# Four small edits to the first head pair and to the minimum of the last queries

## The chip, the core and the metric

The kernel runs on one core of a Trainium2 chip. The metric is the device time of one execution in microseconds (us). The engines are TensorE (PE, with its weight loads as PEld), VectorE (DVE), ScalarE (ACT), GpSimd (POOL) and SyncE (SP, which issues the transfers).

## What is computed

The reference has three stages, in float32. Attention over 4 batches, 8 heads, 1152 positions and head size 64, in which the queries are averaged in pairs, so that 576 queries are left; then a layer of four causal attention experts with a gate that keeps two of four; then a gated convolution layer.

```python
q_pool = q.reshape(B, H, S // 2, 2, D).mean(axis=3)
scores = scale * np.matmul(q_pool, k.transpose(0, 1, 3, 2))
scores = scores - np.max(scores, axis=-1, keepdims=True)
attn = np.exp(scores)
attn = attn / (np.sum(attn, axis=-1, keepdims=True) + 1e-09)
x = np.matmul(attn, v)                      # then (B, 576, 512)
for e in range(4):                          # experts, Hd = 64
    a = softmax(causal(scale * (x @ wq[e]) @ (x @ wk[e]).T))
    out += gate[e] * (a @ (x @ wv[e]) @ wo[e])
gate2 = sigmoid(causal depthwise convolution of out, 5 taps)
return (gate2 * (out @ w_val)) @ w_out
```

## The kernel before

**Order.** Every engine runs its instructions in the order in which the code issues them; there is no scheduler. The first stage follows a string of letters (`ORDER`, line 425) once per pair of heads: S is one piece of scores, T the transposes of a third of a tile, R a row minimum, X an exponential, H the shares, A the product with V. Lists of closures (`late`, `preps`, `begin`) put other work between these.

**First stage.** Sixteen pairs of heads (4 batches x 4) are taken one after the other. A pair has nine tiles of 128 query rows: four for each head and one mixed tile that holds the last 64 queries of both heads. A tile's scores are 128 x 1152 in three groups of 384 keys (`GW`). Each operand is split into a high part, rounded to float32r, and a low part, the rest; `ka` and `kb` (`kst`) hold the keys of the pair's two heads with both parts. For a tile, `scores` (line 436) makes the matmuls (line 451), `rowmin` (line 453) the minimum of the negated scores on VectorE, `expo` (line 458) the exponential with its sum on ScalarE, `transp` (line 492) the transposes (line 500) and their copies (lines 508 and 510), and `av` (line 512) the product with V (line 530), followed by the multiplication with the shares. There are two score buffers, so a tile's scores wait for the exponential two tiles before.

**The first pair** has no pair before it and is prepared in `first()` (line 544) and in the plain loop of line 707. Its queries and keys come twice over, for each head on all partitions (`q0`, `k0`). `qload` and `kload` issue the transfers on SyncE, in this order: for head 0 the queries' first half, the first 384 keys, the other 768 keys; the same for head 1; then the queries' second halves. `kpart(h, g, eng)` makes the high part of a key group on ScalarE (line 584) and the low part on `eng` (line 585). Head 0's three groups are done with VectorE for the low parts; head 1's in `second()` with GpSimd, which is called after the first row minimum. `third()` goes on with the queries' second halves on GpSimd. Before all of this, ScalarE fills parts of two small tiles with zeros (line 347), from a tile that GpSimd sets, and TensorE runs spare matmuls (`spin`, line 617).

**The shares.** After the last exponential of a half of a pair's tiles, `shares` (line 465) adds a small number to the row sums (line 472), takes reciprocals (line 473) and leaves a closure `copies` at the head of `late`. It spreads the reciprocals over 64 or 128 columns of the tile `rm` (lines 478 and 480), which `spread_shares` transposes on TensorE (line 489) at the start of `av`. The copies are made by GpSimd, but for the first half of the first pair by VectorE.

**Second stage.** For each of 4 batches and 2 pairs of experts there are five tiles; `scores2` (line 814) makes the scores, masks them (line 834) and takes the minima (line 835). Tiles 0 to 3 hold 128 queries, and their two banks are the two experts, so two minima are wanted. Tile 4 holds the last 64 queries of both experts (128 rows); its two banks are the two halves of the keys, and a further instruction (line 837) takes the smaller of the two minima. `expo2` (line 839) reads column 0 of `nm` for tile 4. `norm2` (line 850) multiplies the exponentials with the shares on GpSimd (lines 861 and 866).

Of the kernel before, what the change touches and what calls it, by code (L numbers as in the profile page):

```python
# [12 lines left out]
AF = mybir.ActivationFunctionType  # L13
ALU = mybir.AluOpType
AX = mybir.AxisListType
# [5 lines left out]
def tile_kernel(ctx, tc, q, k, v, w_gate, wq, wk, wv, wo, w_val, conv_w, w_out, wo_t, q0, k0, out):  # L21
    nc = tc.nc
    B, H, S, D = v.shape
    P = 128
# [10 lines left out]
    pe, act, dve, pool = nc.tensor, nc.scalar, nc.vector, nc.gpsimd  # L35
# [28 lines left out]
    def f(ap):  # L64
        return ap.bitcast(F32)
# [256 lines left out]
    G = 3  # L322
    GW = 3 * P
# [4 lines left out]
    with ExitStack() as s1:  # L328
# [136 lines left out]
        def shares(m):  # L465

            n, u, i, _ = tiles[m]
            k = len(UNITS[u])
            if i == k - 1:
                rs = st_p.tile([P, 5], F32, name="rs")[:, 0:k]  # L470
                rm = rss[n, u] = rb_p.tile([P, 3, P], F32, name="rm")
                dve.tensor_scalar(rs, sums[(2 * n + u) % len(sums)][:, 0:k], 1e-9, None, op0=ALU.add)
                dve.reciprocal(rs, rs)  # L473
                both = rs[:, 0:4].rearrange("p (h t) -> p t h", h=2)[:, :, :, None].to_broadcast([P, 2, 2, D])

                def copies():
                    eng = pool if n or u else dve
                    eng.tensor_copy(rm[:, 0:2].rearrange("p t (h d) -> p t h d", d=D), both)  # L478
                    if u == 0:
                        eng.tensor_copy(rm[:, 2], rs[:, 4:5].to_broadcast([P, P]))  # L480

                late.insert(0, copies)

# [60 lines left out]
        def first():  # L544

            bufs = pt_p.tile([P, C, 2, 256], F32, name="pt1").rearrange("p c h q -> p (c h q)")
            bufs = [bufs[:, i * S:(i + 1) * S] for i in range(4)]
            kd, qd = bufs[0:2], [t.rearrange("p (c r q) -> p c r q", c=2, r=2) for t in bufs[2:4]]
            vn = v_p1.tile([P, 2, C, D], F32, name="vn")
            kst = [kst_p.tile([P, 2, C * P], F32R, name=n) for n in ("ka", "kb")]  # L550
            data[0] = [qst[0], kst, vn, None]
            def qload(h, c):
                nc.sync.dma_start(qd[h][:, c], q0[h, :, c])

            def kload(h, a, z):
                nc.sync.dma_start(kd[h][:, a:z], k0[h, :, a:z])

            for h in range(2):
                qload(h, 0)
                kload(h, 0, GW)  # L560
                kload(h, GW, S)
            for h in range(2):
                qload(h, 1)

            def qadd(h, c, eng):
                eng.tensor_tensor(out=qd[h][:, c, 0], in0=qd[h][:, c, 0], in1=qd[h][:, c, 1], op=ALU.add)

            def pieces(h, c):
                qp = qd[h][:, c, 0]
                if c == 0:  # L570
                    return [(qst[0][h][:, 0:HQ], qp)]
                return [(last0[h][:, 64 * h:64 * h + 64], qp[:, 4 * P - HQ:]), (qst[0][h][:, HQ:], qp[:, 0:4 * P - HQ])]

            def qhigh(h, c):
                for hi, qp in pieces(h, c):
                    act.activation(hi, qp, AF.Copy, scale=-scale / 2)

            def qlow(h, c, i=0):
                hi, qp = pieces(h, c)[i]
                dve.scalar_tensor_tensor(out=hi[64:P], in0=qp[64:P], scalar=-scale / 2, in1=f(hi[64:P]), op0=ALU.mult, op1=ALU.subtract)  # L580

            def kpart(h, g, eng):
                gs = slice(g * GW, (g + 1) * GW)
                act.activation(kst[h][:, 0, gs], kd[h][:, gs], AF.Copy)
                eng.tensor_tensor(out=kst[h][:, 1, gs], in0=kd[h][:, gs], in1=f(kst[h][:, 0, gs]), op=ALU.subtract)  # L585

            def second():
                kpart(1, 0, pool)
                qhigh(1, 0)
                for g in range(1, G):  # L590
                    kpart(1, g, pool)
                qlow(1, 0)

            def third():
                qadd(1, 1, dve)
                qadd(0, 1, pool)
                for i in range(2):
                    for h in range(2):
                        hi, qp = pieces(h, 1)[i]
                        pool.tensor_scalar(hi, qp, -scale / 2, None, op0=ALU.mult)  # L600

            qadd(0, 0, dve)
            qhigh(0, 0)
            qlow(0, 0)
            kpart(0, 0, dve)

            def rest():
                for g in range(1, G):
                    kpart(0, g, dve)
                qadd(1, 0, dve)  # L610

            return {-1: rest, 0: second, 1: third,
                    2: lambda: (qlow(0, 1), qlow(1, 1), qlow(0, 1, 1)), 3: lambda: qlow(1, 1, 1)}

# [114 lines left out]
        spread, bursts = iter(ends), iter(ends)  # L729
# [78 lines left out]
    with ExitStack() as s2l:  # L808
# [5 lines left out]
        def scores2(s):  # L814
            b, g, i = s
            d = live[s] = {}
            ps = d["ps"] = ps_s2.tile([P, 2, 512], F32, name="s")
            nm = d["nm"] = st_p2.tile([P, 2], F32, name="nm")
            sm = d["sm"] = st_p2.tile([P, 2], F32, name="sm")
            d["p"] = p_p2.tile([P, 2 * 4 * P], F32, name="p")  # L820
            if i < 4:
                w = (i + 1) * P
                for e in range(2):
                    for hl in range(2):
                        pe.matmul(ps[:, e, 0:w], lhsT=qs[g][e][:, i * P:(i + 1) * P], rhs=ks[g][e][:, hl, 0:w], start=hl == 0, stop=hl == 1)  # L825
                dg, mk = ps[:, :, i * P:w], cmask[:, None, :].to_broadcast([P, 2, P])
            else:
                w = HQ
                for c in range(2):
                    ops = [(e, hl) for e in range(2) for hl in range(2)]  # L830
                    for o, (e, hl) in enumerate(ops):
                        pe.matmul(ps[:, c, 0:w], lhsT=qs[g][e][:, 4 * P:], rhs=ks[g][e][:, hl, c * w:(c + 1) * w], start=o == 0, stop=o == 3)  # L832
                dg, mk = ps[:, 1, w - R64:w], cmask2
            dve.tensor_tensor(out=dg, in0=dg, in1=mk, op=ALU.max)
            dve.tensor_reduce(nm, ps[:, :, 0:w], axis=AX.X, op=ALU.min)  # L835
            if i == 4:
                dve.tensor_tensor(out=nm[:, 0:1], in0=nm[:, 0:1], in1=nm[:, 1:2], op=ALU.min)

        def expo2(s):
            b, g, i = s  # L840
# [171 lines left out]
        for n in range(len(steps) + LAG):  # L1012
            if n < len(steps):
                b, g, i = s = steps[n]
# [28 lines left out]
            t = 0.0  # L1043
# [28 lines left out]
            if n < len(steps):  # L1072
                scores2(s)
# [48 lines left out]
    with ExitStack() as s3:  # L1122
# [5 lines left out]
        both = gs_p.tile([P, KT, 2, 2 * SQ], F32R, name="gs")  # L1128
# [102 lines left out]
```

## Time and profile before

| what | value |
|---|---|
| median of 3 runs | 752.74 us (752.27 to 752.74) |
| the profiled execution, its time | 752.01 us |
| its span, first to last instruction | 750.2 us |
| PE busy | 742.2 us, 99% |
| DVE busy | 564.8 us, 75% |
| ACT busy | 447.7 us, 60% |
| POOL busy | 327.4 us, 44% |

Times inside the profile are counted from the span's start. Busy time is the union of an engine's instructions. The chain of work that ended last is followed backwards from the last instruction, at each step to what released it. A timeline row that says x2 joins two neighbouring instructions. The profile does not give each transfer's landing in the timeline; the view of a line gives the least, the median and the greatest time from issue to landing.

### The profile page before, as it was taken

To read this page: it belongs to the slowest core of one execution; us is meant where nothing else is said; L and a number is where in the kernel's file an instruction comes from. 1 tells how busy PE (TensorE), PEld (TensorE's weight loads), DVE (VectorE), ACT (ScalarE), POOL (GpSimd) and SP (SyncE) were. 2 spreads that over 40 slices of the span, in tenths; PEclk is the share of its full clock that TensorE was granted. 3 is DMA by queue.
4 is the path that set the end of the run, shared out by engine and by line. 5 is a ranking of instruction groups with operands and counts; after the bars stand their busy time and mean duration, and the time that the engine had idled before them with its cause. 6 is when DMAs were issued, how large, how long until landed. Compare 5 with 4: busy or idle time off the path is not lost.

```text
span 750.2 us, 14753 instructions
## 1 busy us (share of the span) xinstructions
PE 742.2 (99%) x5317; PEld 616.3 (82%) x5317; DVE 564.8 (75%) x1056; ACT 447.7 (60%) x985; POOL 327.4 (44%) x446
## 2 busy tenths in 40 slices
PE   8999999999999999999999999999999999999998
PEld 7787887787777877877877878889998879888887
DVE  6777898898988988866766667446788889868841
ACT  6666675665656656756657566424574554768442
POOL 6564675675667766743634611012322222336000
DMA  7976878778788597678458484359445553830212
GB/s 263 255 167 202 222 192 254 194 235 252 190 247 255 162 284 220 194 213 244 121 179 227 128 236 162 86 155 212 143 111 128 156 153 73 232 118 15 85 71 84
DMA packets 83784, 133.51 MB, mean 178 GB/s; under 512 B 19072, under 2 KB 55424, under 8 KB 83712
## 3 DMA queue, kind: packets, MB, share of 16 engines
q1 hardware_dynamic: 83712, 132.58, 62.2%
q8 instruction: 42, 0.69, 0.4%
q14 instruction: 30, 0.25, 0.1%
HBM read 53.37 MB, written 21.76 MB: 100 GB/s over the span
## 4 chain that ended last, share of the span: by engine, by line
PE 94%; DMA 2%; DVE 2%; ACT 1%; issue 0%; SPq 0%
PE s L451 21%; PE t L500 19%; PE t L530 19%; PE a L253 7%; PE o L1140 7%; PE a L286 4%; PE a L790 3%; PE a L925 3%; PE a L947 3%; PE s L825 3%; PE a L897 2%; DMA xh<-x_d 2%; PE t L489 1%; PE s L832 1%; PE a L781 1%; DVE nm L456 1%
## 5 line engine op out<-in xcount | busy, mean ns | idle before, releaser
L463 ACT ACTIVATE p<-s,nm 128x1152 f32<-128x1152 f32 x144 | 176.2, 1223 | 87.9 <-DVE nm L456 85.7
L456 DVE TENSOR_REDUCE nm<-s 128x1 f32<-128x1152 f32 x144 | 192.1, 1352 | 14.0 <-PE s L451 13.7
L500 PE MATMUL t<-ident,p 128*128 128x128 f32 x1296 | 199.0, 275 | 0.6 <-DVE xf L532 0.3
L500 PEld LDWEIGHTS t<-ident,p 128*128 128x128 f32 x1296 | 149.0, 141 | 26.5 <-ACT pt L508 7.1
L508 ACT ACTIVATE pt<-t 128x384 f32<-128x384 f32 x223 | 102.2, 490 | 79.8 <-PE t L500 74.9
L530 PE MATMUL t<-pt,vn 128*64 128x256 f32 (+1 forms) x1152 | 146.7, 408 | 0.1
L510 DVE COPY pt<-t 128x384 f32<-128x384 f32 x209 | 110.9, 554 | 44.6 <-PE t L500 40.7
L530 PEld LDWEIGHTS t<-pt,vn 128*64 128x64 f32 x1152 | 80.0, 137 | 56.0 <-issue 5.2
L451 PE MATMUL s<-ka,qst 128*128 128x384 f32 x384 | 114.7, 380 | 0.2 <-DVE ka L585 0.2
L451 PE MATMUL s<-kb,qst 128*128 128x384 f32 x384 | 99.1, 367 | 1.3 <-ACT p L463 1.3
L861 POOL TENSOR_TENSOR p<-p,sm 128x512 f32<-128x512 f32 (+3 forms) x32 | 40.1, 1254 | 101.4 <-DVE sm L859 63.3
L451 PEld LDWEIGHTS s<-kb,qst 128*128 128x128 f32 x384 | 60.9, 189 | 15.3 <-issue 13.1
L451 PEld LDWEIGHTS s<-ka,qst 128*128 128x128 f32 x384 | 62.9, 190 | 1.3 <-DVE ka L585 0.9
L478 POOL COPY rm<-rs 128x256 f32<-128x256 f32 x31 | 12.4, 399 | 79.0 <-DVE rs L473 77.8
L388 POOL TENSOR_TENSOR hlk<-kt,hlk 128x384 fp32r<-128x384 f32 x45 | 45.4, 1009 | 1.1
L532 DVE TENSOR_TENSOR xf<-t,rb 128x320 f32<-128x320 f32 (+1 forms) x32 | 14.6, 456 | 41.2 <-PE t L530 40.4
L539 POOL CAST xt<-xf 128x320 fp32r<-128x320 f32 (+1 forms) x32 | 13.6, 425 | 70.5 <-DVE xf L532 69.9
L253 PE MATMUL a<-xh,wqk 128*128 128x288 f32 x288 | 43.4, 299 | 0.7 <-DMA xh<-x_d 0.7
L846 ACT ACTIVATE p<-s,nm 128x256 f32<-128x256 f32 (+3 forms) x64 | 33.1, 526 | 16.2 <-DVE nm L835 16.2
L253 PEld LDWEIGHTS a<-xh,wqk 128*128 128x128 f32 x288 | 39.5, 188 | 2.0 <-DMA xh<-x_d 1.2
L226 DVE SCALAR_TENSOR_TENSOR gp<-x,cw,gp 128x572 f32<-128x572 f32 (+3 forms) x48 | 38.7, 810 | 2.7 <-ACT gp L950 2.1
L451 PE MATMUL s<-hlk,mixed 128*128 128x384 f32 x135 | 33.7, 357 | 0.0
(190 smaller groups left out, 1174.0 us busy)
## 6 DMA issues: line engine op xcount, KB each, us to landing
ka<-hlk SPq DMA_DIRECT2D x90, 192.0 KB, 3.2
kb<-hlk SPq DMA_DIRECT2D x90, 192.0 KB, 3.7
vn<-in_v_dram SPq DMA_DIRECT2D x16, 576.0 KB, 7.2
k<-hl SPq DMA_DIRECT2D x32, 288.0 KB, 4.9
kt<-in_k_dram SPq DMA_DIRECT2D x15, 576.0 KB, 6.1
qt<-in_q_dram SPq DMA_DIRECT2D x15, 576.0 KB, 5.3
qst<-hlq SPq DMA_DIRECT2D x60, 128.0 KB, 3.1
xh<-x_d SPq DMA_DIRECT2D x12, 576.0 KB, 6.6
```

The source lines that it names most:

```text
L226: dve.scalar_tensor_tensor(out=gp[:, n:], in0=x[:, 0:SQ - n], scalar=cw[:, m, c:c + 1], in1=gp[:, n:], op0=ALU.mult, op1=ALU.add)
L253: pe.matmul(ps[:, 0:HQ], lhsT=wqk[wi][:, t, cs], rhs=xh[t][xi][:, qsl], start=o == 0, stop=o == len(ops) - 1)
L388: late.append(lambda: pool.tensor_tensor(out=hlk[:, 1, gs], in0=kt[:, gs], in1=f(hlk[:, 0, gs]), op=ALU.subtract))
L451: pe.matmul(ps[:, 0:GW], lhsT=ops[c][0], rhs=ops[c][1], start=c == 0, stop=c == len(ops) - 1)
L456: dve.tensor_reduce(d["nm"], d["s"][:, :, 0:GW], axis=AX.XY, op=ALU.min)
L463: act.activation(d["p"], d["s"][:, :, 0:GW], AF.Exp, bias=d["nm"], scale=-1.0, accum_out=sums[(2 * n + u) % len(sums)][:, i:i + 1])
L500: pe.transpose(ps[:, j * P:(j + 1) * P], p[:, g, j * P:(j + 1) * P], ident)
L508: act.activation(dst, src, AF.Copy)
L510: dve.tensor_copy(dst, src)
L530: pe.matmul(ps[64 * h:64 * h + 64, 0:N], lhsT=vn[:, h, j, :], rhs=pt[:, j, h, :], start=j == 0, stop=j == C - 1)
L861: pool.tensor_tensor(out=pv, in0=pv, in1=sm[:, :, None].to_broadcast([P, 2, w]), op=ALU.mult)
L1140: pe.matmul(ps[:, 0:w], lhsT=hl[xi][:, kt, t * P - a:(t + 1) * P - a], rhs=end3["wo3"][:, kt, wi, c:c + w], start=o == 0, stop=o == len(op ...
```

## The change

Four edits. The first 384 keys of the first pair's head 0 are issued by ScalarE and not by SyncE, at the same place in the code. The high part of the last key group of head 1 is made by GpSimd and not by ScalarE: GpSimd now makes it after the low part of the group before the last two, and ScalarE makes two high parts there. The two copies of the shares in the first half of the first pair are made by ScalarE and not by VectorE. In the second stage the minimum of tile 4 is one reduction over both banks into column 0; the second instruction goes.

```diff
                 def copies():
-                    eng = pool if n or u else dve
-                    eng.tensor_copy(rm[:, 0:2].rearrange("p t (h d) -> p t h d", d=D), both)
+                    spread = [(rm[:, 0:2].rearrange("p t (h d) -> p t h d", d=D), both)]
                     if u == 0:
-                        eng.tensor_copy(rm[:, 2], rs[:, 4:5].to_broadcast([P, P]))
+                        spread.append((rm[:, 2], rs[:, 4:5].to_broadcast([P, P])))
+                    for dst, src in spread:
+                        if n or u:
+                            pool.tensor_copy(dst, src)
+                        else:
+                            act.activation(dst, src, AF.Copy)
...
             def kload(h, a, z):
-                nc.sync.dma_start(kd[h][:, a:z], k0[h, :, a:z])
+                queue = act if h == a == 0 else nc.sync
+                queue.dma_start(kd[h][:, a:z], k0[h, :, a:z])
...
             def second():
                 kpart(1, 0, pool)
                 qhigh(1, 0)
-                for g in range(1, G):
-                    kpart(1, g, pool)
+                pool.tensor_copy(kst[1][:, 0, 2 * GW:], kd[1][:, 2 * GW:])
+                kpart(1, 1, pool)
+                pool.tensor_tensor(out=kst[1][:, 1, 2 * GW:], in0=kd[1][:, 2 * GW:], in1=f(kst[1][:, 0, 2 * GW:]), op=ALU.subtract)
                 qlow(1, 0)
...
             dve.tensor_tensor(out=dg, in0=dg, in1=mk, op=ALU.max)
-            dve.tensor_reduce(nm, ps[:, :, 0:w], axis=AX.X, op=ALU.min)
-            if i == 4:
-                dve.tensor_tensor(out=nm[:, 0:1], in0=nm[:, 0:1], in1=nm[:, 1:2], op=ALU.min)
+            if i < 4:
+                dve.tensor_reduce(nm, ps[:, :, 0:w], axis=AX.X, op=ALU.min)
+            else:
+                dve.tensor_reduce(nm[:, 0:1], ps[:, :, 0:w], axis=AX.XY, op=ALU.min)
```

## Rows read from the trace of the kernel before

**Rows 1.** The page: span, busy time by engine, chain that ended last by engine.
```profile
span 750.2 us, 14753 instructions
...
PE 742.2 (99%) x5317; PEld 616.3 (82%) x5317; DVE 564.8 (75%) x1056; ACT 447.7 (60%) x985; POOL 327.4 (44%) x446
...
PE 94%; DMA 2%; DVE 2%; ACT 1%; issue 0%; SPq 0%
```

**Rows 2.** The chain that ended last, 0 to 60 us: start, length, what.
```profile
1.63 4.51 DMA pt<-in_k_dram
...
15.16 1.31 PE s L451 x6
```

**Rows 3.** Line 556, the four key transfers: issue durations (ns), starts; time to landing.
```profile
L556 SPq DMA_DIRECT2D pt<-in_k_dram x4: 416/428/432, 1.2 to 3.0; - x4
...
DMA to landing us min/median/max: 2.9/4.7/5.3
```

**Rows 4.** Timeline of ACT, 0 to 12 us: start, length, instruction, [idle before <- releaser].
```profile
2.87 0.40 ACT L347 ACTIVATE last<-zero 128x64 fp32r<-128x64 f32 x2 [0.88 <-POOL zero L62]
...
6.17 0.94 ACT L584 ACTIVATE ka<-pt 128x384 fp32r<-128x384 f32 x2 [1.23 <-DMA pt<-in_k_dram]
...
8.50 0.92 ACT L584 ACTIVATE kb<-pt 128x384 fp32r<-128x384 f32 x2
```

**Rows 5.** Timeline of DVE, 3 to 11 us.
```profile
6.72 1.03 DVE L585 TENSOR_TENSOR ka<-pt,ka 128x384 fp32r<-128x384 f32 x2 [1.12 <-ACT ka L584]
...
8.29 1.36 DVE L456 TENSOR_REDUCE nm<-s 128x1 f32<-128x1152 f32 x1 [0.17 <-PE s L451]
```

**Rows 6.** Timeline of POOL, 7 to 26 us.
```profile
8.06 3.19 POOL L585 TENSOR_TENSOR kb<-pt,kb 128x384 fp32r<-128x384 f32 x3 [4.54 <-ACT kb L584]
...
14.79 0.50 POOL L387 CAST hlk<-kt 128x384 fp32r<-128x384 f32 x1
...
23.44 1.42 POOL L402 TENSOR_TENSOR hlq<-qp,hlq 128x576 fp32r<-128x576 f32 x1
```

**Rows 7.** Timeline of PE, 7 to 16 us.
```profile
11.05 1.32 PE L451 MATMUL s<-kb,qst 128*128 128x384 f32 x6 [1.08 <-ACT p L463]
```

**Rows 8.** Stretches: us, busy by engine (instructions), granted clock, DMA share, GB/s.
```profile
10.00:11.00 1.00, 0.00 (x0) 0.00 (x0) 0.97 (x2) 0.99 (x2) 1.00 (x2) 1.00 0.98 394
```

**Rows 9.** Timeline of DVE, 22.5 to 28 us.
```profile
23.56 1.33 DVE L472 TENSOR_SCALAR rs<-sums 128x5 f32<-128x5 f32 x1
...
25.15 0.29 DVE L478 COPY rm<-rs 128x256 f32<-128x256 f32 x1
...
25.59 0.54 DVE L510 COPY pt<-t 128x384 f32<-128x384 f32 x1
```

**Rows 10.** Timeline of ACT, 23 to 30 us.
```profile
27.50 1.22 ACT L463 ACTIVATE p<-s,nm 128x1152 f32<-128x1152 f32 x1 [2.84 <-DVE nm L456]
...
28.71 0.37 ACT L522 ACTIVATE rb<-t 128x256 f32<-128x256 f32 x1
```

**Rows 11.** Timeline of PE, 25.2 to 26.3 us.
```profile
25.00 0.51 PE L451 MATMUL s<-kb,qst 128*128 128x384 f32 x2
25.59 0.52 PE L489 MATMUL t<-ident,rm 128*128 128x128 f32 x3
26.19 0.49 PE L530 MATMUL t<-pt,vn 128*64 128x320 f32 x2
```

**Rows 12.** Line 837: durations (ns, least/median/greatest), first and last start.
```profile
L837 DVE TENSOR_TENSOR nm<-nm x8: 180/684/686, 510.4 to 666.6; 128x1 f32<-128x1 f32 x8
```

**Rows 13.** Timeline of DVE, 574.1 to 577.7 us, one of the eight tiles.
```profile
575.56 0.69 DVE L837 TENSOR_TENSOR nm<-nm 128x1 f32<-128x1 f32 x1
```

**Rows 14.** Timeline of POOL, 574.1 to 577.7 us.
```profile
574.76 1.47 POOL L861 TENSOR_TENSOR p<-p,sm 128x768 f32<-128x768 f32 x1 [4.48 <-DVE s L834]
```

**Rows 15.** Both waits of PE, 490 to 700 us: line, releaser, total us, times, longest.
```profile
PE a L253 <- DMA xh<-x_d: 0.7, 1, 0.7
PE s L825 <- DMA q<-hl: 0.2, 1, 0.2
```

## The prediction

> **What bounds the kernel now.** I read the page first: TensorE (PE) is busy for 99% of the span, and the chain that ended last is 94% PE [rows 1]. So an edit counts only where PE itself stands still, and I looked for such places near the four edits. In the chain's first rows the reader should see that the front is different: until 15.16 us the chain runs from a transfer over ScalarE (ACT), VectorE (DVE) and short PE pieces, and from 15.16 us on it is nearly all PE [rows 2]. A shift D of the front is therefore carried, unhidden, to the end. The one transfer in the chain is the second piece of head 0's keys, 4.51 us from 1.63 to 6.14 [rows 2]. The first piece is not in the chain: issued at 1.17, it landed 2.9 us later, near 4.05, and the four key pieces took 2.9 us (the first) to 5.3 us (the last, issued near 3.05) [rows 3].
>
> **Part 1, the first key piece on ACT's queue.** SP loses one issue of 0.42 us [rows 3], so all its later issues come some 0.46 us sooner. ACT's program has the two fills of line 347 in front of the new issue; they ran from 2.87 to 3.27, held by GpSimd's (POOL's) zero [rows 4]. So the piece leaves at about 3.2, not 1.17. The issue itself (0.42 us, until about 3.7) hides in the gap before ACT's next work at 4.08 (line 576, released by DVE). What is queued behind the piece's landing T on ACT is everything: its own high part (line 584), the high parts of pieces two and three, those of head 1, and the first exponential.
>
> Before, the second landing at 6.15 started two high parts on ACT (0.94 us for two) [rows 4], their two low parts on DVE (1.03 us for two), and the first row minimum started at 8.29 [rows 5]: 2.14 us after the landing. With T last there are three pieces instead of two, at DVE's pace of 1.03/2 = 0.52 us, so the row minimum starts at T + 2.66. The shift is D = T + 2.66 - 8.29 = T - 5.63.
>
> T is not in the trace. The low end is 3.0 + 2.9 = 5.9, the latency that this very piece had with only one transfer in front of it; a landing much quicker than that is shown by no row of that time. The high end is a piece that takes its place behind all that SP has issued: the last key piece, which now has the same bytes in front as the moved one would have, landed at 3.05 + 5.3 = 8.35 [rows 3]. I take T = 6.3, the low end plus 0.4 for sharing the transfer engines with SP's backlog, because a queue of its own has nothing else in it. D = +0.67; ends +0.27 and +2.72.
>
> A rule speaks against this part: the Trainium skill, "DMA: Bandwidth & Descriptors", section "Issuing engines are not separate DMA queues", says that all issuers' transfers run on the same sixteen engines and that a second issuer saves only issue time, usually small. Its section "Queues, rings and completion order" says that each engine takes the rings in turn; by that the piece would not wait out SP's backlog, and the sum would stay near the low end. No row here shows two queues at once.
>
> **Part 2, one high part on POOL.** ACT loses half of 0.92 us (the two at 8.50) [rows 4]; it was waiting for the row minimum afterwards, so nothing is gained on the path. POOL gets a 128x384 copy, 0.50 us by its own copy at 14.79, between its three low parts, which ran from 8.06 to 11.25 [rows 6]. Against the row minimum POOL starts about 0.2 earlier (head 1's first high part follows the third of head 0 on ACT directly) and ends about 0.3 later: 3.2 us after the row minimum's start. The third group's low part is needed by the last of six matmuls that begin at 11.05, 2.8 us after that start [rows 7], at about 3.8. Cover 0.6 us; cost nothing. If the cover were gone, it would cost at most 0.5. POOL's next work, up to pair 1's keys, slides with it by 0.3.
>
> **Part 3, the shares' copies on ACT.** Before, DVE made two copies from 25.15 and only then the last transposed block, 25.59 to 26.13 [rows 9], for which the A.V matmuls waited until 26.19 [rows 11]. PE's losses there: the last score matmul starts near 25.17 (two in 0.51 us, 0.17 apart), so the transposes of the shares could start at 25.35 but did at 25.59; three of them 0.12 apart would let A.V start at 25.95 but it did at 26.19. Together up to 0.48 us. On ACT the copies cover an idle stretch (2.84 us before 27.50); the nearest price is 0.37 us for 128x256 [rows 10], the smaller at most as much. Copies ready at 25.15 + 0.37 hold the first transpose until about 25.6, as now, and the last until about 25.85; DVE's block is ready near 25.7. A.V then starts near 26.0: gain 0.2. No operation behind it on ACT is due before 27.4.
>
> DVE's sum of shares (line 472, 128x5) took 1.33 us, from 23.56 to 24.89 [rows 9], and POOL's subtraction ended at 24.86 [rows 6]: it was held. If POOL's 0.3 us slide lets the small operation go first, the shares are ready over 1 us sooner and all 0.48 is gained; if it is held by the shifted one, POOL ends 0.3 later and about 0.1 is lost. I take -0.3; ends -0.48 and +0.1. The Trainium skill, "SBUF — State Buffer", section "Who interferes with whom", says that a pair of ports is shared by DVE and POOL, that whoever is first keeps it for its whole instruction, and that issue order decides. Line 472's end 0.03 us behind POOL's agrees; by this rule the result would be the 0.48.
>
> **Part 4, one instruction for the minimum.** Eight tiny minima (line 837, median 0.68 us) go [rows 12]. They were held too: one ends at 576.25 [rows 13], POOL's multiply at 576.23 [rows 14]. The new one-value form exists already over 1152 elements at 1.36 us [rows 5]; over 576 it is taken at half of that, and I take it as no dearer than the reduction that it replaces. DVE is relieved of about 7 x (0.68 + 0.03) + 0.2 = 5.2 us, and ACT's exponential comes up to 0.6 us sooner. But in this stretch PE's only two listed waits, 0.7 and 0.2 us, are for transfers, none is for DVE or ACT [rows 15]. Cost 0; ends -0.5 (small holds inside the PE pipeline that no row shows) and 0.
>
> **Sum.** +0.67 + 0 - 0.3 + 0 = +0.37 us. The profiled execution has a span of 750.2 us [rows 1] and took 752.01; it would take about 752.4. The median of the runs shown is 0.73 above that execution, 752.74; the forecast is 753.1. Its own ends: +0.27 - 0.48 - 0.5 = -0.7 (752.0), and, for T up to 7.2, +1.6 + 0.1 (754.4).
>
> **The rivals.**
> Slower, the backlog: the moved piece waits behind what SP has issued. Place: ACT at its first line 584. T = 8.35 gives D = +2.7, with part 3 +2.4: 755.1. It decides from T = 7.4 on (+1.5 net). For it: transfers at this time land 4.5 to 5.3 us after issue [rows 2, 3]. Against it: that is the backlog of one queue, and this is another. Chance 0.14.
> Slower, the clock: PE's first scores need the moved piece, which lands at 6.3 instead of 4.05, so PE stands idle some 2 us longer behind its warm-up. If the clock fell from 2.4 to 1.2 GHz, the two groups of six matmuls (1.32 us the first [rows 7]) before PE takes the lead would each take about 1 us longer: +1 to +2, 754.1 to 755.1. Against it: 1.08 us of idleness before 11.05 left the granted clock at 1.00 [rows 7, 8], the upper level. Chance 0.05.
> It doesn't do what it says, to the good: the issue isn't held by the fills and the piece lands by 5 us. Then the second piece is the last, its issue 0.46 sooner: -0.46 - 0.3, 752.0. Against it: program order on ACT. Chance 0.05.
> Faster by part 4: DVE's 5.2 us turn into PE time in part; up to a third of it, -1.4 net, 751.4. Against it: PE's listed waits name no DVE [rows 15]. Chance 0.05.
>
> **How the numbers follow.** Forecast 0.71; the rivals 0.14, 0.05, 0.05, 0.05. 0.2% is 1.5 us, about what a measurement of this kernel can tell from no change. Slower than 754.2: the backlog, most of the clock's case, a sliver of the forecast's tail: 0.19. Faster than 751.2: the far end of part 4's case and little else: 0.03. The rest is 0.78. The range takes the forecast's own ends and reaches up to the backlog's 755.1: 752.0 to 755.2.
>
> **What would show it.** Right: the key transfer issued on ACT near 3.2 us; ACT's first line 584 released by it near 6.3; the first row minimum near 9.0 instead of 8.29; the same shift still at 15.16; A.V's start shifted by less than that; line 837 gone and PE's waits after 490 us unchanged. Wrong: the issue near 0.7 or 2 us; a landing beyond 7.4; matmul pieces before 16 us that last twice as long; a shift at 490 us that differs from that at 31 us.

## The result and the profile after

| what | before | after |
|---|---|---|
| median | 752.74 us | 759.59 us (5 runs, 758.69 to 759.85) |
| ratio | | 1.0091, 95% interval 1.0081 to 1.0102 |
| the profiled execution | 752.01 us | 758.69 us |
| its span | 750.2 us | 756.9 us |
| DVE busy | 564.8 us | 561.7 us |
| start of the first row minimum | 8.29 us | 15.55 us |

The change makes the kernel slower by 6.85 us, 0.9%. The page of the changed kernel, the lines that answer to [rows 1], with the row of the granted clock (in tenths of full speed, 40 equal slices of the span), which the page before does not have:

```profile
span 756.9 us, 14744 instructions
...
PE 743.1 (98%) x5317; PEld 618.5 (82%) x5317; DVE 561.7 (74%) x1046; ACT 446.7 (59%) x986; POOL 328.0 (43%) x447
...
PEclk8999999999999999999999999999999999999999
...
PE 94%; DMA 3%; DVE 2%; ACT 1%; issue 0%; SPq 0%
```

PE has nearly the same work (743.1 for 742.2 us) in a longer span, and the only slice in which the clock is not full is the first. The chain that ended last, 0 to 40 us, answers to [rows 2]; its columns are start, length, what:

```profile
1.16 3.40 DMA pt<-in_k_dram
...
4.58 6.49 DMA pt<-in_k_dram
...
15.55 1.37 DVE nm L456
...
22.41 1.31 PE s L451 x6
```

Two transfers stand in the chain, one after the other: the second key piece until 4.56 us, and from 4.58 on the moved first piece, 6.49 us long. PE takes the lead at 22.41 instead of 15.16. Following the same PE instructions through both traces, the delay is 7.3 us at the first row minimum, 6.9 at the first A.V, 6.9 at 460 us, 7.1 at 490 and 6.7 at the end: it is made in the front and then carried. The front on ACT, 0 to 17 us, answers to [rows 4]:

```profile
2.87 0.40 ACT L347 ACTIVATE last<-zero 128x64 fp32r<-128x64 f32 x2 [0.88 <-POOL zero L62]
4.58 0.38 ACTq L561 DMA_DIRECT2D pt<-in_k_dram  x1
5.06 0.44 ACT L581 ACTIVATE qst<-pt 128x288 fp32r<-128x288 f32 x1 [1.79 <-DMA pt<-in_k_dram]
11.09 1.35 ACT L589 ACTIVATE ka<-pt 128x384 fp32r<-128x384 f32 x3 [5.59 <-DMA pt<-in_k_dram]
```

The issue (line 561, marked ACTq) does not follow the fills at 3.28; it comes at 4.58, when the second piece has landed. Even the query work behind it (line 581, ready at 4.0) waits for that. Then ACT has nothing for 5.59 us. The list of the changed program's instructions names the wait, which stands in no line of the source (shortened):

```
ACT   L347 ACTIVATE last<-zero
ACT   L561 DMA pt<-in_k_dram 128x384   [waits DMAHW1]
...
ACT   L589 ACTIVATE ka<-pt 128x384     [waits DMAHW1]
...
SP    L365 DMA kt<-in_k_dram
SP    L366 DMA vn<-in_v_dram           [waits DMAHW0]
SP    L367 DMA qt<-in_q_dram           [waits DMAHW2]
```

The framework counts landings on eight semaphores, DMAHW0 to 7, for both issuing engines together, and gives them out in the order in which it expects the issues. Eight of SP's come first; the ninth (line 366) takes number 0 again, and ACT's, taken for the tenth, takes number 1. That is the second key piece's, so the issue has to wait until that piece has landed (4.56 us). The start of the row minimum, DVE, 5 to 17 us, answers to [rows 5], PE's first scores, 10 to 19 us, to [rows 7], and the granted clock in three stretches to [rows 8] (the clock stands third from the end):

```profile
11.65 1.50 DVE L590 TENSOR_TENSOR ka<-pt,ka 128x384 fp32r<-128x384 f32 x3 [5.65 <-ACT ka L589]
13.06 1.25 DVE L571 TENSOR_TENSOR pt<-pt 128x288 f32<-128x288 f32 x1
15.55 1.36 DVE L456 TENSOR_REDUCE nm<-s 128x1 f32<-128x1152 f32 x1 [1.23 <-PE s L451]
```
```profile
11.67 1.28 PE L451 MATMUL s<-ka,qst 128*128 128x384 f32 x2 [6.15 <-ACT ka L589]
```
```profile
7.00:8.50 1.50, 0.00 (x0) 0.00 (x0) 0.00 (x0) 0.00 (x0) 0.00 (x0) 1.00 1.01 374
9.00:15.00 6.00, 3.33 (x12) 3.03 (x13) 2.67 (x4) 2.41 (x6) 1.68 (x2) 0.50 0.96 377
15.60:20.00 4.40, 3.41 (x24) 3.19 (x23) 4.10 (x5) 2.32 (x3) 3.38 (x6) 1.00 0.00 0
```

After the spare matmuls PE had nothing to do from 5.5 to 11.7 us. In this pause the granted clock fell from 1.00 to 0.50, the lower of its two levels (1.2 and 2.4 GHz), and it was back at 1.00 only after 15 us. The row minimum waits 1.23 us for PE, where it waited 0.17 before.

### The profile page after: what moved, and what is told of

It reads as the page before. It is cut to its first block, busy times and chain, and to the rows that moved or that the text cites. A ratio compares the mean times of both kernels' runs of the same rounds, so it can differ in the third digit from the quotient of the medians.

```text
span 756.9 us, 14744 instructions
## 1 busy us (share of the span) xinstructions
PE 743.1 (98%) x5317; PEld 618.5 (82%) x5317; DVE 561.7 (74%) x1046; ACT 446.7 (59%) x986; POOL 328.0 (43%) x447
## 4 chain that ended last, share of the span: by engine, by line
PE 94%; DMA 3%; DVE 2%; ACT 1%; issue 0%; SPq 0%
PE s L451 22%; PE t L504 19%; PE t L534 19%; PE a L253 7%; PE o L1147 7%; PE a L286 4%; PE a L796 3%; PE a L932 3%; PE a L954 3%; PE s L831 3%; PE a L904 2%; DMA xh<-x_d 2%; DMA pt<-in_k_dram 1%; PE t L493 1%; PE s L838 1%; PE a L787 1%
## 5 line engine op out<-in xcount | busy, mean ns | idle before, releaser
L482 POOL COPY rm<-rs 128x256 f32<-128x256 f32 (+1 forms) x46 | 15.9, 364 | 78.4 <-DVE rs L473 75.5
```

## The experiments

My theory after the result: the whole loss comes from the moved transfer. Its issue is held by the shared semaphore, the piece then lands behind all that SP has issued, and the pause lets PE's clock fall. Rivals: the other three edits carry part of it; a second queue shares the engines in turn, and only the hold is at fault; a transfer on ACT's queue is slow in itself; the clock costs nothing on top of the landing.

**The move alone** (part1_alone), on the kernel before:

```diff
-                nc.sync.dma_start(kd[h][:, a:z], k0[h, :, a:z])
+                queue = act if h == a == 0 else nc.sync
+                queue.dma_start(kd[h][:, a:z], k0[h, :, a:z])
```

> The kernel before with the moved key transfer alone. If the move accounts for the whole loss: ACT's issue is held until the second piece's landing near 4.6 us, the piece lands near 11.1, the first row minimum starts near 15.5 as with all four edits, and the time is 759.6 to 760.0 (a few tenths more than with all four, since part 3's small gain is missing). If the other three edits carry a good part of the loss: below 757.

Measured: 759.96 us, ratio 1.0097 (1.0081 to 1.0112). Issue at 4.59, landing at 11.11, row minimum at 15.58 (DVE, 5 to 17 us):

```profile
15.58 1.36 DVE L456 TENSOR_REDUCE nm<-s 128x1 f32<-128x1152 f32 x1 [1.23 <-PE s L451]
```

The move accounts for all of the loss.

**The other three parts** (parts234): the changed kernel with `queue = nc.sync` throughout.

> The changed kernel with all key transfers on SP again, so parts 2 to 4 alone. If the move accounts for the whole loss: first row minimum at 8.3 as before, A.V of the first pair 0.1 to 0.3 us sooner against the scores in front of it, nothing after 490 us: 752.2 to 752.7. If the other edits carry a good part of the loss: above 754.

Measured: 752.44 us, ratio 0.999 (0.9982 to 0.9999): no loss, at most a gain that is smaller than 0.2%. In its trace DVE, 24 to 27 us, and PE, 26 to 27.2 us, answer to [rows 9, 11]:

```profile
24.76 0.39 DVE L472 TENSOR_SCALAR rs<-sums 128x5 f32<-128x5 f32 x1
25.18 0.19 DVE L473 RECIPROCAL rs<-rs 128x5 f32<-128x5 f32 x1
26.05 0.56 DVE L514 COPY pt<-t 128x384 f32<-128x384 f32 x1 [0.68 <-PE t L504]
```
```profile
25.77 0.96 PE L451 MATMUL s<-kb,qst 128*128 128x384 f32 x4
26.57 0.49 PE L493 MATMUL t<-ident,rm 128*128 128x128 f32 x3
26.98 0.49 PE L534 MATMUL t<-pt,vn 128*64 128x320 f32 x2
```

Line 472 took 0.39 us instead of 1.33, and the way from the four score matmuls' start to A.V is 1.21 us; before it was 1.62 (24.57 to 26.19). That is 0.41 us, near the 0.48 which the prediction gave if the small operation went first.

The same trace shows part 2 on the path. Head 1's first keys landed at 8.32 in this execution, and the chain that ended last goes from there through GpSimd, with the new high part (line 594) in it, to the third row minimum:

```profile
9.01 1.01 POOL kb L589
10.02 0.45 POOL kb L594
...
11.63 0.99 POOL kb L596
...
12.66 0.46 PE s L451
...
13.15 1.37 DVE nm L456
```

The third row minimum starts 4.53 us after the first (8.62); before it was 4.11 (8.29 to 12.40). By the 3.19 us of [rows 6], GpSimd would have ended near 12.2 without the new high part (an estimate), before PE's last score matmul needed it. So part 2 cost some 0.4 us here.

**The issue first** (issue_first): ScalarE's fills of line 347 are put behind the transfers in its program, so that the issue is ACT's first instruction.

```diff
-            act.activation(last0[h][:, 64 - 64 * h:128 - 64 * h], zero, AF.Copy)   # line 347
...
             for h in range(2):
                 qload(h, 1)
+            for h in range(2):
+                act.activation(last0[h][:, 64 - 64 * h:128 - 64 * h], zero, AF.Copy)
```

> The changed kernel with ScalarE's two zero fills put behind the transfers in its program, so that its issue is its first instruction and waits for nothing. If the loss comes from the late issue: issue near 0.7 us, landing near 4, the second piece near 5.5 to 6.1 is the last again, first row minimum 7.7 to 8.3, time 751.8 to 752.6. If a transfer on ACT's queue is slow in itself (6.5 us from issue to landing, as in the changed kernel): landing near 7.2, first row minimum near 9.9, time 754 or more.

Measured: 753.04 us, ratio 0.9999 (0.9991 to 1.0008), a little above the expected 751.8 to 752.6, and the first row minimum at 8.62, above the expected 7.7 to 8.3. The moved issue on ACT, 0 to 8 us, and DVE's first work, 3 to 11 us:

```profile
0.71 0.40 ACTq L560 DMA_DIRECT2D pt<-in_k_dram  x1
```
```profile
4.70 0.46 DVE L572 TENSOR_TENSOR pt<-pt 128x288 f32<-128x288 f32 x1 [4.70 <-DMA pt<-in_q_dram]
...
8.62 1.36 DVE L455 TENSOR_REDUCE nm<-s 128x1 f32<-128x1152 f32 x1 [0.60 <-PE s L450]
```

Issued at the same moment as the first queries, the piece landed 4.2 us later, so ACT's queue is not slow in itself. But the queries, which started DVE at 3.59 before, now come at 4.70: the two transfers slow each other, and what SP saves in issuing (the second piece landed near 5.7 instead of 6.15) is lost again. Even with an issue that is not held, the move gained nothing here.

**PE kept at work** (warm): `spin(9)` becomes `spin(38)` in the changed kernel.

> The changed kernel with 38 spare matmuls instead of 9 in front, so that PE works until the late piece lands. If the fall of the clock costs 1.8 us on top of the landing: granted clock 1.0 in the whole front, landing near 11.1 as before, first row minimum near 13.7 (landing plus 2.66) instead of 15.55, time near 757.8. If the landing alone sets the front: 15.5 and 759.6 again.

Measured: 757.9 us, ratio 1.0063 (1.005 to 1.0077), 1.7 us less than the changed kernel and as expected; the first row minimum came at 14.70, a full 1 us later than expected. Two stretches, and DVE, 11 to 16 us:

```profile
9.00:11.00 2.00, 2.00 (x21) 2.00 (x20) 0.00 (x0) 0.00 (x0) 0.00 (x0) 1.00 1.02 401
11.00:13.00 2.00, 2.00 (x18) 1.83 (x17) 0.91 (x2) 1.47 (x4) 0.00 (x0) 1.00 1.04 416
```
```profile
13.50 1.27 DVE L571 TENSOR_TENSOR pt<-pt 128x288 f32<-128x288 f32 x1
14.70 1.34 DVE L456 TENSOR_REDUCE nm<-s 128x1 f32<-128x1152 f32 x1
```

The clock stays at 1.00. In this execution the piece landed at 11.51, so the row minimum starts 3.19 us after the landing; in the changed kernel it was 4.48. So the clock cost 1.29 us up to the first row minimum. Against the predicted 2.66 there are 0.53 left. The row minimum starts here without a wait for PE: DVE's own work in front of it ended last, and of that line 571 took 1.27 us, where the same operation (line 566, at 7.67) took 0.45 before. Why it took longer is not shown.

**No shared semaphore** (fewer_transfers): head 1's queries and keys come in one transfer each, so that ACT's issue takes a fresh semaphore.

```diff
-            for h in range(2):
-                qload(h, 0)
-                kload(h, 0, GW)
-                kload(h, GW, S)
-            for h in range(2):
-                qload(h, 1)
+            qload(0, 0)
+            kload(0, 0, GW)                      # on ACT
+            kload(0, GW, S)
+            nc.sync.dma_start(qd[1], q0[1])
+            kload(1, 0, S)
+            qload(0, 1)
```

> The changed kernel with head 1's queries and keys in one transfer each, so that ACT's issue no longer shares a semaphore with an earlier transfer and waits only for the zero fills: issue near 3.3 us. If the piece waits behind the bytes that SP has issued by then (2112 KB in front; the seventh transfer of the changed kernel, with the same bytes in front, landed at 9.06): landing 8.9 to 9.5, first row minimum 11.6 or, with the clock's fall, up to 13.5, time 756 to 758. If two queues share in turn and only the held issue was at fault: landing 6.2 to 6.6, first row minimum near 9, time 752.8 to 753.5.

Measured: 758.03 us, ratio 1.0072 (1.0057 to 1.0087). ACT, 0 to 11 us:

```profile
2.88 0.38 ACTq L561 DMA_DIRECT2D pt<-in_k_dram  x1
...
9.76 1.35 ACT L589 ACTIVATE ka<-pt 128x384 fp32r<-128x384 f32 x3 [5.34 <-DMA pt<-in_k_dram]
```

and the landings of line 561, first of ACT's issue, then of SP's issue of head 1's keys at 2.1 us:

```profile
DMA to landing us min/median/max: 6.9/6.9/6.9
```
```profile
L561 SPq DMA_DIRECT2D pt<-in_k_dram x1: 431/431/431, 2.1 to 2.1; - x1
...
DMA to landing us min/median/max: 8.2/8.2/8.2
```

The view of the transfers counts the packets of each queue; q1 is SP's and q10, which the kernel before does not have, is ACT's. First from 2.9 to 6.4 us, then from 6.4 to 9.5:

```profile
q1 hardware_dynamic: 357, 1.24, 97.8%
```
```profile
q1 hardware_dynamic: 279, 0.87, 79.9%
q10 hardware_dynamic: 144, 0.20, 21.0%
```

The columns are packets, MB and share of the 16 engines. The row minimum (DVE, 5 to 17 us), and the granted clock in a stretch:

```profile
14.21 1.36 DVE L456 TENSOR_REDUCE nm<-s 128x1 f32<-128x1152 f32 x1 [1.23 <-PE s L451]
```
```profile
9.50:15.00 5.50, 4.66 (x16) 4.36 (x17) 3.45 (x5) 2.62 (x6) 2.73 (x4) 0.50 0.96 377
```

The issue is not held: it goes at 2.88, while the fills still run. The piece lands at 9.74 all the same, 0.5 us before a transfer that SP issued 0.8 us earlier (2.1 + 8.2 = 10.3). Sharing in turn from the issue on was expected to bring it by 6.6. The packets show why it did not: ACT's queue moved none until 6.4 us, 3.5 us after the issue, while SP's moved 1.24 MB; from then on both queues moved packets side by side. In the changed kernel it is the same: no packet of ACT's queue from the issue at 4.58 until 8.4, all 144 between 8.4 and 10.7, beside 0.74 MB of SP's. So the queues do share, but a transfer issued behind a backlog joins in late; what holds it until then no view shows. The backlog theory's 8.9 to 9.5 was a little short (the transfer it was taken from had 1824 KB in front, this piece 2112 KB), and so was the time, 756 to 758: the row minimum started 4.47 us after the landing, as in the changed kernel, for the clock fell here too.

**Its base** (fewer_sp): the same with all transfers on SP.

> The same kernel with all transfers on SP, as the base for fewer_transfers: second piece of head 0's keys near 6.15 to 6.5, first row minimum near 8.3 to 8.6, time 752.2 to 752.8, by either theory.

Measured: 754.65 us, ratio 1.0028 (1.0017 to 1.0039), and the expectation missed by 2 us. Head 1's keys in one piece land late, and the third tile waits for them (ACT, 6 to 17 us). PE pauses for 1.7 us before 12.48, and the clock is low afterwards:

```profile
9.96 0.52 ACT L589 ACTIVATE kb<-pt 128x384 fp32r<-128x384 f32 x1 [2.02 <-DMA pt<-in_k_dram]
```
```profile
13.90:17.20 3.30, 2.95 (x12) 2.85 (x12) 2.81 (x6) 2.06 (x4) 2.96 (x6) 0.50 0.40 157
```

So fewer_transfers has a loss of its own of about 2 us, and against this base the move without the hold costs 3.4 us (758.03 less 754.65).

**The same place, issued by SP** (late_on_sp): the changed kernel, with the moved piece issued by SP between the first two transfers of pair 1.

```diff
             if n == 1:
                 nc.sync.dma_start(kt, k[b, hp])
+                then()                           # kload(0, 0, GW) on SP
                 nc.sync.dma_start(data[0][2], v[0, 0:2].rearrange("h (p c) d -> p h c d", p=P))
```

> The changed kernel with the moved piece issued by SP, behind pair 1's keys and so at the same late time (near 4.5 us) as ACT issued it. If the place in the backlog decides and not the issuer: landing 11.2 to 11.8, first row minimum near 15.6, time 759 to 760, as in the changed kernel. If ACT's queue made the piece slower than SP's would: a landing clearly before 11.

Measured: 759.2 us, ratio 1.009 (1.0069 to 1.011). Its line 561 and ACT, 4 to 13 us:

```profile
L561 SPq DMA_DIRECT2D pt<-in_k_dram x1: 753/753/753, 4.7 to 4.7; - x1
...
DMA to landing us min/median/max: 6.7/6.7/6.7
```
```profile
11.48 1.35 ACT L591 ACTIVATE ka<-pt 128x384 fp32r<-128x384 f32 x3 [7.06 <-DMA pt<-in_k_dram]
```

Issued at 4.7 by SP it took 6.7 us, issued at 4.6 by ACT 6.5. The moment of issue decides here, not the issuer.

**Parts 3, 2 with 3, and 4 alone**, each on the kernel before, with the lines of the change's diff.

> The kernel before with the shares' copies on ScalarE alone. By the sum of the prediction: line 472 is held by GpSimd as before (ends about 0.03 us behind GpSimd's subtraction), the copies take 0.4 and 0.3 us on ScalarE, A.V of the first pair comes 0.1 to 0.2 us sooner against the scores in front of it, time 752.3 to 752.8. If the copies on ScalarE are late instead: A.V 0.1 later or more.

> Parts 2 and 3 together, on the kernel before. If GpSimd's 0.3 us slide lets line 472 go first, as the looks at parts234 showed (0.39 us instead of 1.33): line 472 under 0.5 us, A.V 0.4 sooner against the scores in front, time 752.0 to 752.5. If it is held again, as in the changed kernel: 1.3 us, A.V 0.1 to 0.2 sooner, 752.3 to 752.8.

> The kernel before with the one-instruction minimum alone. If PE's lead hides it: line 837 gone, DVE some 5 us less busy, the exponentials of tile 4 up to 0.6 us sooner, PE's waits after 490 us unchanged at 0.7 and 0.2, time within 0.3 of before (752.3 to 752.9). If DVE's time counts in the second stage: 751.5 or less.

Measured: ratios 1.0008 (0.9993 to 1.0024), 1.0003 (0.9991 to 1.0015) and 1.0004 (0.9991 to 1.0017); medians 752.41, 752.32 and 752.19 beside 752.29 for the kernel before. None moves the time by more than can be told. The profile of part3_alone is of an execution of 1048 us and is not read, so what the copies alone do to A.V stays unshown. With parts 2 and 3 line 472 took 0.40 us. The profiled execution of parts23 (755.58 us) lost some 4 us near 520 us, where PE waited for transfers of the second stage. For part 4, the new reduction (line 838) and PE's waits from 490 to 705 us answer to [rows 12, 15]:

```profile
L838 DVE TENSOR_REDUCE nm<-s x8: 757/757/757, 509.8 to 666.3; 128x1 f32<-128x576 f32 x8
```
```profile
PE a L253 <- DMA xh<-x_d: 0.7, 1, 0.7
PE s L825 <- DMA q<-hl: 0.5, 1, 0.5
```

## Why the prediction was wrong

**What bounds the kernel: right.** The front is a chain before PE takes the lead, and a shift of it is carried nearly whole to the end: 7.3 us at the first row minimum, 6.7 at the end.

**Part 1, the moment of the issue: wrong, the first step that failed.** The prediction took 3.2 us, behind the fills. The issue was held until 4.58 by a semaphore that it shares with the second key piece. The fills were not the limit: in fewer_transfers, with a semaphore of its own, the issue went at 2.88. The trace of before had the sign of the shared semaphores: two of SP's later issues, the eleventh and the twelfth (lines 367 and 371), went only at 6.16 and 6.88, just behind the landings of its third and fourth transfer. I had seen these stops and did not ask what they were; they are the same eight semaphores going round.

**Part 1, the landing T: wrong, the step that cost most.** I took 6.3, near the low end, "because a queue of its own has nothing else in it". It was 11.07. fewer_transfers separates the two errors: not held, and issued at 2.88, the piece still landed at 9.74. So the wrong belief about the queue is worth 3.4 us of T, and the hold about 1.3 more, though the two kernels do not have the same transfers in front.

The high end of 8.35 was too low as well. It gave the last key piece the same bytes in front as the moved one, but by the sizes of the transfers that piece had 1344 KB in front, and an issue at 3.2 us would have had 1824 KB. At the 394 GB/s of [rows 8] the missing 480 KB are some 1.2 us more (an estimate).

Two rules stood beside this step. The Trainium skill, "DMA: Bandwidth & Descriptors", section "Queues, rings and completion order", says that each engine takes the rings in turn. The trace agrees from 6.4 us on in fewer_transfers, where both queues move packets in the same stretch; my reading, that the piece would therefore not wait out the backlog, was wrong, for in the 3.5 us before ACT's queue moved nothing. The same page of the Trainium skill, section "Issuing engines are not separate DMA queues", says that a second issuer saves issue time alone. issue_first agrees: the second piece came some 0.45 us sooner, the first queries 1.1 us later.

**The rule D = T - 5.63: too small, mostly by the clock.** With T = 11.07 it gives 5.44, a row minimum at 13.73; it started at 15.55, 1.82 later. By warm 1.29 of this is the clock's; the other 0.53 stays with the clock up, and its cause in the changed kernel is open. I had given the clock a chance of 0.05 and a price of 1 to 2 us. The price was about right (1.29 in the traces, 1.7 in the medians), its place was wrong: I set it beside the late landing, as another way for things to go. It is a consequence of it: the later the piece, the longer PE's pause, and the idle 1.08 us of [rows 7], which left the clock up, said nothing of a pause of 6 us.

**The rivals came together.** The backlog and the clock each stood in my text with an end near 755, and the range was drawn as if only one of them could happen. But even the two ends together, +2.4 and +2, would have given 757.1, short of the measured 759.59; the rest is the hold and the high end that was too low.

**Part 2: right in the time, wrong about the cover.** The cost was put at nothing behind a cover of 0.6 us. parts234 shows the cover gone when head 1's keys land later, and a cost of some 0.4 us in the front, within the 0.5 that the prediction named for that case. In the changed kernel the third row minimum comes 4.10 us after the first, as before, and the time of parts 2 with 3 (1.0003) shows no loss.

**Part 3: within its ends, not told in the time.** -0.3 was taken between -0.48 and +0.1. In the changed kernel line 472 was held again, and the way from the scores to A.V was 1.49 us (31.56 to 33.05) for 1.62, a gain of 0.13 (DVE, 30 to 36 us; PE, 31.5 to 33.5 us):

```profile
30.53 1.32 DVE L472 TENSOR_SCALAR rs<-sums 128x5 f32<-128x5 f32 x1
```
```profile
31.56 0.94 PE L451 MATMUL s<-kb,qst 128*128 128x384 f32 x4
...
33.05 0.76 PE L534 MATMUL t<-pt,vn 128*64 128x320 f32 x4
```

In parts234 and parts23 the small operation went first, and the gain was 0.4. In the changed kernel GpSimd's subtraction (30.39 to 31.82) started 0.14 us before line 472; in parts234 it started after it, at 25.21. So the order of the two goes with the result, as the prediction said. No experiment changes that order alone.

**Part 4: right in the time.** The reduction takes the same 0.757 us for one value as for two, line 837 is gone, and PE still waits for the same two transfers only. DVE was relieved of 3.5 us in part4_alone (561.3 busy for 564.8), not of the 5.2 that were forecast, and this is worth nothing that can be measured.

**The best version** is not told from the kernel before with any certainty: parts234 has 0.999 of its time, with an interval that just leaves 1 out; parts 2 with 3 and part 4 by themselves do not confirm a gain.

## What to carry to other kernels

In these runs a transfer that was moved to another engine's queue did not start fresh: behind a backlog its first packet moved 3.5 to 3.8 us after the issue, and it took about as long to land as from SP (6.5 and 6.7 us). A piece that is needed first should be issued first, whoever issues it. Look in the built program for the wait that the move adds on the issuing engine; a pool of semaphores shared by both queues can tie an issue to a transfer with which it has nothing to do. And when a wait lets TensorE stop, price the clock in the same case, not in a rival of its own.

## What the runs showed of the hardware

Issued by ACT with some 1.8 MB of SP's transfers still to move in front (an estimate from the sizes issued and the bytes moved by then), 192 KB took 6.5 us to land in the changed kernel and 6.9 in fewer_transfers; the same piece issued by SP at nearly the same moment took 6.7. Its packets moved only in the last part of this time, from 8.4 us (changed kernel) and 6.4 us (fewer_transfers) on, and then beside SP's. Issued together with SP's first transfer, with nothing in front, it took 4.2 us, and SP's first one 4.0 instead of 2.8.

A transfer's issue on ACT can go while the activations in front of it still run (2.88 us in fewer_transfers, with the fills from 2.87 to 3.28).

A pause of PE from 5.5 to 11.7 us brought the granted clock from 1.00 to 0.50, and it was back at 1.00 only in the stretch from 15.6 us, when PE had gone through the first scores and some spare matmuls at the lower level. In fewer_sp it stood at 0.50 from 13.9 to 17.2 us, after a pause of 1.7 us.
